# Top-32 attention and an ELU feed-forward block on one core: gates shared between two engines, a written prologue, and weights decoded at another pace

## The chip, the cores and the metric

The kernel runs on one core of a Trainium2 chip. The metric is device time in microseconds (us), from repeated runs of the same program. Five engines work side by side, each through its own queue in order: TensorE (PE, with its weight loads as PEld), VectorE (DVE), ScalarE (ACT), GpSimd (POOL) and SyncE (SP), which issues most DMAs.

## The reference, cut to what matters

There are 8 batches, 8 heads, 576 positions and a head dimension of 64. Each query keeps only its 32 largest scores. The output of attention, 4608 tokens of 512 values, goes through a feed-forward block (FFN) with 2048 hidden values and an ELU between its two products. q, k and v are float32; the weights arrive as float64 words and are turned into float32 on the chip.

```python
scores = scale * np.matmul(q, k.transpose(0, 1, 3, 2))
kth = np.partition(scores, -top_k, axis=-1)[..., -top_k:-top_k + 1]
scores = np.where(scores >= kth, scores, -1000000000.0)
scores = scores - np.max(scores, axis=-1, keepdims=True)
attn = np.exp(scores)
attn = attn / (np.sum(attn, axis=-1, keepdims=True) + 1e-09)
x = np.matmul(attn, v)        # heads side by side: (4608, 512)
...
h = x @ w_in
g = np.where(h > 0.0, h, np.exp(np.minimum(h, 0.0)) - 1.0)
return g @ w_out
```

## The kernel before

**Steps.** The attention is cut into 144 steps, each one tile of 128 query rows for a pair of heads: per batch four full tiles (`qt` 0 to 3) for four head pairs, and a remainder of 64 rows per head (`qt` 4) in two steps. For one step, `scores` (L291) makes the scores on PE and ACT copies them to SBUF; `select_row` (L313) or `select` (L334) finds the 32nd largest value of each row on DVE, for each of two heads with four MAX8 and three MATCH_REPLACE8 over 576 columns; `mask` (L357) turns scores into weights with POOL's `neg` and `gap` and two ACT passes; `normalise` (L374) divides on POOL; `turn` (L391) transposes on PE, with ACT's copies; `attend` (L416) multiplies by v on PE, and `finish` (L453) copies the result into `xT`, the FFN's input. These parts of one step are spread over the loop's steps: scores are made two steps ahead, mask and normalise come one step later, the turn two steps later.

**Order.** The first eight steps (`tight`, L541) are left to the language's own scheduler, which orders each engine's instructions by priority. From step 8 on the loop is under `manual_schedule` (L666): PE, ACT, DVE and POOL execute in the order in which the program is written, and a step is cut into quarters by `next(passes)`.

**FFN.** Tokens are gathered into 19 blocks of one, two or three slots of 128 tokens. When a block's `xT` is complete, its pieces are queued: 16 `hidden` pieces (L478), each four matmuls into a PSUM tile, two ACT Relu's of it (`n` of the negative part, `g` of the positive), an ACT Exp of `n`, and a gate that has to follow; then four `project` pieces per slot (L507), each four of 16 matmuls. `feed` (L601) is called in every quarter step and lets out as many pieces as a plan of costs and due times asks for, so that PE's FFN work is spread evenly. A piece is held back until the number of decoded weights, `decoded`, is high enough: for block 0 in stages, for every later block until all 32 are decoded.

**Gates.** The gate `g = g + n - 1` completes the ELU. It runs on DVE (L471), put off by `close_gates(2)` in `feed` for two quarters; a `hidden` piece closes the oldest if more than three are open, and a `project` piece closes all. `n` has five buffers (four for block 0).

**Decoding.** Each of 32 weight pieces (128 x 512 float64, 512 KB) is loaded by SP (`load_weight`, L150) into a raw tile of four parts: the low and high words interleaved, `e` and `m`. `convert_first` (L159) runs three ACT passes (L169 to L171) and a POOL clamp (L172); `convert_last` (L176) runs two DVE instructions (L179, L182) and a POOL integer add (L186) into the weight tile. `decode_piece` (L204) loads piece i+2, runs the first half of piece i and the last half of piece i−1. `hook` (L193) takes the next of 33 such pieces. It is called twice for each head's row in steps 0 to 7, four times a step, so that the last piece falls in step 8. When all are done the raw tiles are given up and the FFN's late buffers take their place. Three raw tiles exist.

**Prologue.** Before the loop, q and k of two head pairs are loaded (each six DMAs on SP), with the first two weights in between, and the scores of steps 0 and 1 are made, in the scheduler's order.

Of the kernel before, what the change touches and what calls it, by code (L numbers as in the profile page):

```python
# [12 lines left out]
I32 = mybir.dt.int32  # L13
# [67 lines left out]
def kernel(  # L81
# [27 lines left out]
    def pool(name, bufs, **kw):  # L109
        return ctx.enter_context(tc.tile_pool(name=name, bufs=bufs, **kw))  # L110
# [5 lines left out]
    wkpool = pool("wk", 1)  # L116
    etpool = pool("et", 2)
    small = pool("small", 4)
    xtpool = pool("xt", 2)
    opool = pool("o", 1)  # L120
    ps_sc = pool("ps_sc", 1, space=PSUM)
    ps_t = pool("ps_t", 2, space=PSUM)
# [3 lines left out]
    raws = ExitStack()  # L126
    early = raws.enter_context(tc.tile_pool(name="early", bufs=1))
    earlyf = raws.enter_context(tc.tile_pool(name="earlyf", bufs=4))
    rawpool = raws.enter_context(tc.tile_pool(name="raw", bufs=3))

    ident = const.tile([P, P], FP32, tag="ident", name="ident")
    make_identity(nc, ident[:])
# [15 lines left out]
        return moe_w_out[f * P : (f + 1) * P, :], w_out[:, f, :]  # L148

    def load_weight(i):  # L150
        t = rawpool.tile([P, 4 * WN], U32, tag="raw", name="raw")
        nc.sync.dma_start(t[:, 0 : 2 * WN], weight(i)[0])
        raw[i] = t

    def parts(t):
        words = t[:, 0 : 2 * WN].rearrange("p (n w) -> p n w", w=2)
        return words[:, :, 0], words[:, :, 1], t[:, 2 * WN : 3 * WN], t[:, 3 * WN :]

    def convert_first(i):  # L159

        lo, hi, e, m = parts(raw[i])
        ef, mf = e.bitcast(FP32), m.bitcast(FP32)
        nc.scalar.activation(ef, hi.bitcast(FP32), AF.Abs, scale=2.0**-48)  # L169
        nc.scalar.activation(mf, lo, AF.Copy, scale=2.0**-29, bias=2.0**23)  # L170
        nc.scalar.activation(m.bitcast(I32), mf, AF.Copy, bias=-(2.0**23))  # L171
        nc.gpsimd.tensor_scalar(  # L172
            ef, ef, (2.0 - 2.0**-3 - 2.0**-23) * 2.0**-32, 2.0**-63, ALU.min, ALU.max
        )

    def convert_last(i):  # L176
        t, dst = raw.pop(i), weight(i)[1]
        lo, hi, e, m = parts(t)
        nc.vector.tensor_scalar(  # L179
            e, e, 0x0FFFFFFF, 3, ALU.bitwise_and, ALU.logical_shift_left  # L180
        )
        nc.vector.scalar_tensor_tensor(  # L182
            out=e, in0=hi, scalar=0x80000000, in1=e,
            op0=ALU.bitwise_and, op1=ALU.bitwise_or,
        )
        nc.gpsimd.tensor_tensor(  # L186
            dst.bitcast(I32), e.bitcast(I32), m.bitcast(I32), ALU.add
        )

    decode = []  # L190
# [2 lines left out]
    def hook():  # L193

        if not decode:
            return
        decode.pop(0)()
        if not decode:
            raws.close()
            late["f"] = ctx.enter_context(tc.tile_pool(name="f", bufs=5))  # L200
            late["g"] = ctx.enter_context(tc.tile_pool(name="g", bufs=2))
            late["x"] = ctx.enter_context(tc.tile_pool(name="x", bufs=2))

    def decode_piece(i):  # L204
        if i < 2 * NF:
            if i + 2 < 2 * NF:
                load_weight(i + 2)
            convert_first(i)
        if i > 0:
            convert_last(i - 1)  # L210
            decoded[0] = i

    loaded, kqT, vT = {}, {}, {}

    def load_qk(b, hp):

        for name, src in (("k", k), ("q", q)):
            n = J + 1 if name == "k" else J
            t = ldpool.tile([P, n, 2, D], FP32, tag=name + "in", name=name + "in")
            if name == "k":  # L220
                last = t
            for hh in range(2):
                nc.sync.dma_start(
                    t[:, 0:J, hh, :],
                    src[b, 2 * hp + hh, 0:JP, :].rearrange("(p j) d -> p j d", j=J),
                )
            nc.sync.dma_start(
                last[0:R, J, :, :] if name == "k" else last[R:P, J, :, :],
                src[b, 2 * hp : 2 * hp + 2, JP:S, :].rearrange("h p d -> p h d"),
            )  # L230
            loaded[b, hp, name] = t
# [47 lines left out]
    def start_qk(b, hp):  # L279
        turning.append(transpose_qk(b, hp))  # L280
# [32 lines left out]
    def select_row(u, i):  # L313
        if i == 0:
            u.first = small.tile([P, 2, 8], FP32, tag="m1", name="m1")
            u.last = small.tile([P, 2, 8], FP32, tag="m4", name="m4")
        sc = u.sc[:, i, :]
        m = u.first[:, i, :]
        nc.vector.max(m, sc)
        wk = wkpool.tile([P, S], FP32, tag=f"wk{i}", name="wk")  # L320
        cur = sc
        for r in range(TOP_K // 8 - 1):
            nc.vector.match_replace(wk[:], m, cur, TAKEN)  # L323
            cur = wk[:]
            if r < TOP_K // 8 - 2:
                m = small.tile([P, 8], FP32, tag=f"m{i}", name="m")[:]
            else:
                m = u.last[:, i, :]
            nc.vector.max(m, cur)  # L329
            if r != 1:  # L330
                hook()
                yield

    def select(u):  # L334

        u.first = small.tile([P, 2, 8], FP32, tag="m1", name="m1")
        u.last = small.tile([P, 2, 8], FP32, tag="m4", name="m4")
        cur = [u.sc[:, i, :] for i in range(2)]
        found = [u.first[:, i, :] for i in range(2)]
        for i in range(2):  # L340
            nc.vector.max(found[i], cur[i])  # L341
        yield
        wk = [wkpool.tile([P, S], FP32, tag=f"wk{i}", name="wk")[:] for i in range(2)]
        for r in range(TOP_K // 8 - 1):
            for i in range(2):
                nc.vector.match_replace(wk[i], found[i], cur[i], TAKEN)  # L346
            cur = wk
            for i in range(2):
                if r < TOP_K // 8 - 2:
                    found[i] = small.tile([P, 8], FP32, tag=f"m{i}", name="m")[:]  # L350
                else:
                    found[i] = u.last[:, i, :]
                nc.vector.max(found[i], cur[i])  # L353
            hook()
            yield
# [96 lines left out]

    def finish(blk, parts, at, cols, src):  # L453
        if blk.xT is None:
            if blk.slots == 1 and late:
                blk.xT = late["x"].tile([P, NC, P], FP32, tag="xT", name="xT")
            else:
                blk.xT = xtpool.tile([P, NC, T], FP32, tag="xT", name="xT")
        nc.scalar.copy(blk.xT[:, at, cols], src)
        blk.left -= parts  # L460
        if blk.left == 0:
            ffn.extend(ffn_pieces(blk))
# [1 line left out]
    gates = []  # L464
    place = [0]

    def close_gates(keep=0):

        while gates and gates[0][0] <= place[0] - keep:
            _, dst, n = gates.pop(0)  # L470
            nc.vector.scalar_tensor_tensor(  # L471
                out=dst, in0=n, scalar=-1.0, in1=dst, op0=ALU.add, op1=ALU.add
            )

    def ffn_pieces(blk):
        n_tok = blk.slots * P

        def hidden(f):  # L478
# [4 lines left out]
                g = late["g"].tile([P, NG, T], FP32, tag="g", name="gT")  # L483
                blk.gT.append(g[:])
            if len(gates) > 3:
                gates[0] = (-1, *gates[0][1:])
                close_gates(place[0])
            ps = ps_f.tile([P, dm], FP32, tag="f", name="hps")
            for i in range(NC):
                nc.tensor.matmul(  # L490
# [11 lines left out]
            nc.scalar.activation(n, ps[:, 0:n_tok], AF.Relu, scale=-1.0)  # L502
            nc.scalar.activation(g, ps[:, 0:n_tok], AF.Relu)  # L503
            nc.scalar.activation(n, n, AF.Exp, scale=-1.0)  # L504
            gates.append((place[0], g, n))

        def project(s, part):  # L507
            close_gates()
            if part == 0:
                blk.o = ps_f.tile([P, dm], FP32, tag="f", name="ops")  # L510
            step = NF // 4
            for f in range(part * step, (part + 1) * step):
                nc.tensor.matmul(  # L513
                    blk.o[:],
                    blk.gT[f // NG][:, f % NG, s * P : (s + 1) * P],
                    w_out[:, f, :],
                    start=(f == 0),
                    stop=(f == NF - 1),
                )
            if part == 3:  # L520
                o = opool.tile([P, dm], FP32, tag="osb", name="osb")
                nc.scalar.copy(o[:], blk.o[:])
                for t in blk.tiles[s]:
                    p0 = t.cols.start - s * P
                    nc.sync.dma_start(out[t.rows, :], o[p0 : p0 + t.ql, :])
# [87 lines left out]
            fed["sum"] += cost  # L613
            piece()

    load_qk(0, 0)
    for i in range(2):
        load_weight(i)
    load_qk(0, 1)
    load_v(0, 0)  # L620
    start_qk(0, 0)
    turn_qk(True)
    scores(steps[0])
    load_qk(0, 2)
    start_qk(0, 1)
    turn_qk(True)
    scores(steps[1])
    load_qk(0, 3)
    for hp in range(1, NHP):
        load_v(0, hp)  # L630
    decode += [lambda i=i: decode_piece(i) for i in range(2 * NF + 1)]
    at(0, start_qk, 0, 2)
    at(1, start_qk, 0, 3)

# [5 lines left out]
    for n in range(NS + 3):  # L640
# [20 lines left out]
                feed(n, 0.25)  # L661
            continue
        if n == tight:
            E = mybir.EngineType
            ctx.enter_context(
                tc.manual_schedule(engines={E.PE, E.Activation, E.DVE, E.Pool})  # L666
            )
        passes = select(cur) if cur else iter(range(4))
        if ahead:
            scores(ahead)  # L670
# [59 lines left out]
```

## Time and profile before

| what | us |
|---|---|
| median of 3 runs | 1694.59 (1694.2 to 1695.28) |
| the profiled execution's own time | 1695.23 |
| its span, first to last instruction | 1693.4 |
| busy: PE / DVE / ACT / POOL | 1597.5 / 1542.7 / 1179.6 / 627.0 |
| first MAX8 of step 0 on DVE | 15.91 |
| DVE begins step 9, 10, 11 | 164.43, 174.07, 184.23 |
| gates on DVE (L471) | 304, 129.1 busy |
| weight decoding on DVE (L179, L182) | 64, 45.7 busy |

The profile is of one execution. An engine is counted as busy while it executes; DMA issues, branches and semaphores don't count. Rows of instructions give the line, the engine, the operation, output and input with their shapes, the number, and busy time, mean duration and the idle time before them with what ended it. In views of stretches each line has the stretch, its length and each engine's busy time with its number of instructions, then the granted TensorE clock, the DMA share and GB/s.

### The profile page before, as it was taken

The numbers are of one execution on the slowest core, as the hardware profiler recorded it, in microseconds if no ns is written. First come the engines' busy times: TensorE is split into PE (matmuls) and PEld (weight loads), VectorE is DVE, ScalarE is ACT, GpSimd is POOL, SyncE is SP. The second block draws the span as 40 slices with busy tenths as digits, with TensorE's granted clock in tenths as the row PEclk, the third lists the DMA queues.
The fourth block names the chain that finished last, engine by engine and source line by source line (L and its number), as shares of the span: only waits on it lengthen the run. The fifth ranks groups of instructions, "written<-read, shape, count | busy, mean of one in ns | idle before, by whom it ended". The sixth has DMA issues, their size and how long they took to land.

```text
span 1693.4 us, 26805 instructions
## 1 busy us (share of the span) xinstructions
PE 1597.5 (94%) x8560; PEld 1035.0 (61%) x8560; DVE 1542.7 (91%) x3248; ACT 1179.6 (70%) x2813; POOL 627.0 (37%) x1719
## 2 busy tenths in 40 slices
PE   4568899999999999999999999999999999999999
PEld 3355676667575666756557575755557575755565
DVE  6889999999999999999999999999998999998600
ACT  5787776778776776857758585867758686857531
POOL 3675333343333333433333333333333333332200
PEclk8568999999999999999999999999999999999999
DMA  5531021001200111001100111001100000000000
GB/s 156 169 130 63 15 56 36 7 1 42 51 12 7 29 35 42 1 14 42 43 19 1 28 42 35 7 10 46 36 20 8 21 21 28 7 7 7 7 13 13
DMA packets 101131, 56.25 MB, mean 33 GB/s; under 512 B 84096, under 2 KB 92288, under 8 KB 100992
## 3 DMA queue, kind: packets, MB, share of 16 engines
q1 hardware_dynamic: 100992, 54.55, 11.7%
q8 instruction: 68, 1.11, 0.3%
q14 instruction: 71, 0.58, 0.1%
HBM read 45.09 MB, written 9.44 MB: 32 GB/s over the span
## 4 chain that ended last, share of the span: by engine, by line
PE 68%; DVE 21%; ACT 5%; issue 2%; POOL 2%; DMA 1%; SPq 0%; ACTq 0%; POOLq 0%; DVEq 0%
PE ops L513 25%; PE hps L490 21%; PE avps L432 8%; DVE wk L346 7%; PE scps L300 7%; DVE m L353 6%; PE eps L406 5%; DVE m L341 2%; DVE gT L471 1%; DVE wk L323 1%; DVE m L329 1%; PE qkps L270 1%; ACT sc L370 1%; ACT sc L369 1%; ACT et L407 1%
## 5 line engine op out<-in xcount | busy, mean ns | idle before, releaser
L353 DVE MAX8 m<-wk 128x8 f32<-128x576 f32 x816 | 574.9, 745 | 0.0
L490 PE MATMUL hps<-xT,w_in 128*128 128x256 f32 (+2 forms) x2432 | 554.3, 376 | 19.3 <-ACT gT L503 19.3
L513 PE MATMUL ops<-w_out,gT 128*128 128x512 f32 x1152 | 522.6, 598 | 0.0
L490 PEld LDWEIGHTS hps<-xT,w_in 128*128 128x128 f32 x2432 | 409.5, 194 | 119.9 <-ACT gT L503 26.4
L346 DVE MATCH_REPLACE8 wk<-m,wk 128x576 f32<-128x576 f32 x544 | 399.4, 741 | 0.0
L513 PEld LDWEIGHTS ops<-w_out,gT 128*128 128x128 f32 x1152 | 208.4, 190 | 232.8 <-issue 201.0
L380 POOL TENSOR_SCALAR dene<-den 128x2 f32<-128x2 f32 x144 | 34.9, 243 | 819.6 <-ACT sc L370 819.0
L369 ACT ACTIVATE sc<-sc,neg 128x576 f32<-128x576 f32 x288 | 226.5, 787 | 56.6 <-POOL neg L366 56.1
L370 ACT ACTIVATE sc<-sc,gap 128x576 f32<-128x576 f32 x288 | 223.2, 775 | 26.6 <-ACT sc L369 1.9
L308 ACT ACTIVATE sc<-scps 128x576 f32<-128x576 f32 x288 | 173.4, 661 | 82.4 <-PE scps L300 82.4
L387 POOL TENSOR_SCALAR sc<-sc,rec 128x576 f32<-128x576 f32 x288 | 218.7, 769 | 15.2 <-POOL rec L385 0.4
L300 PE MATMUL scps<-kqT 64*128 64x288 f32 (+1 forms) x1280 | 198.1, 438 | 21.5 <-ACT sc L308 14.7
L471 DVE SCALAR_TENSOR_TENSOR gT<-n,gT 128x256 f32<-128x256 f32 (+2 forms) x304 | 129.1, 431 | 95.3 <-ACT n L504 95.3
L407 ACT COPY et<-eps 128x512 f32<-128x512 f32 x288 | 167.4, 581 | 61.8 <-PE eps L406 61.8
L406 PEld LDWEIGHTS eps<-ident,sc 128*128 128x128 f32 x1152 | 144.5, 145 | 93.4 <-issue 48.9
L346 DVE MATCH_REPLACE8 wk<-m,sc 128x576 f32<-128x576 f32 x272 | 199.7, 741 | 0.0
L432 PE MATMUL avps<-et,vT 128*64 128x256 f32 (+2 forms) x2080 | 191.0, 325 | 9.0 <-ACT et L407 8.4
L406 PE MATMUL eps<-ident,sc 128*128 128x128 f32 x1152 | 177.9, 280 | 21.8 <-POOL sc L387 18.6
L341 DVE MAX8 m<-sc 128x8 f32<-128x576 f32 x272 | 191.3, 744 | 0.0
L432 PEld LDWEIGHTS avps<-et,vT 128*64 128x64 f32 x2080 | 122.3, 140 | 80.4 <-issue 24.7
L502 ACT ACTIVATE n<-hps 128x256 f32<-128x256 f32 (+2 forms) x304 | 112.6, 370 | 84.2 <-PE hps L490 79.0
L300 PEld LDWEIGHTS scps<-kqT 64*128 64x128 f32 (+1 forms) x1280 | 106.0, 180 | 90.2 <-issue 45.1
(47 smaller groups left out, 1236.6 us busy)
## 6 DMA issues: line engine op xcount, KB each, us to landing
kin<-in_k_dram SPq DMA_DIRECT2D x64, 128.0 KB, 2.8
qin<-in_q_dram SPq DMA_DIRECT2D x64, 128.0 KB, 2.8
raw<-in_moe_w_in_dram SPq DMA_DIRECT2D x16, 512.0 KB, 3.9
vT<-in_v_dram SPq DMA_DIRECT2D x64, 128.0 KB, 2.3
raw<-in_moe_w_out_dram SPq DMA_DIRECT2D x16, 512.0 KB, 3.3
out_dram<-osb SPq DMA_DIRECT2D x32, 256.0 KB, 2.2
kin<-in_k_dram SPq DMA_DIRECT2D x32, 32.0 KB, 2.5
kin<-in_q_dram SPq DMA_DIRECT2D x32, 32.0 KB, 2.2
```

The source lines that it names most:

```text
L300: nc.tensor.matmul(wide[i][rows, half, 0:HS], kq[part, q0 : q0 + u.t.ql], kq[part, k0 : k0 + HS], start=True, stop=True,)
L341: nc.vector.max(found[i], cur[i])
L346: nc.vector.match_replace(wk[i], found[i], cur[i], TAKEN)
L353: nc.vector.max(found[i], cur[i])
L369: nc.scalar.activation(sc, sc, AF.Prelu, bias=neg[:], alpha=STEEP)
L370: nc.scalar.activation(sc, sc, AF.Exp, bias=gap[:], accum_out=u.den[:, i : i + 1])
L387: nc.gpsimd.tensor_scalar(u.sc[:, i, :], u.sc[:, i, :], rec[:, i : i + 1], 1.0, ALU.mult, ALU.mult)
L406: nc.tensor.transpose(ps[:, c * P : (c + 1) * P], sc[:, c0 : c0 + P], ident[:])
L407: nc.scalar.copy(g.et[:, chunks, u.at, :], ps[:, 0 : n * P].rearrange("p (c q) -> p c q", c=n),)
L432: nc.tensor.matmul(ps[i * D : (i + 1) * D, cols], vt[:, 2 * J + i if c == J else i * J + c, :], w, start=(c == 0), stop=(c == J),)
L490: nc.tensor.matmul(ps[:, 0:n_tok], w_in[:, i, f * P : (f + 1) * P], blk.xT[:, i, 0:n_tok], start=(i == 0), stop=(i == NC - 1),)
L513: nc.tensor.matmul(blk.o[:], blk.gT[f // NG][:, f % NG, s * P : (s + 1) * P], w_out[:, f, :], start=(f == 0), stop=(f == NF - 1),)
```

## The change

- Every second gate, those with an odd number `f`, runs on POOL as two instructions. A `project` piece closes only the gates that it reads, and a full list closes only its oldest. `n` has four late buffers in place of five.
- The prologue's transposes and first scores of steps 0 and 1 are under `manual_schedule`, before the other q and k loads; q of the first head pair is loaded from ACT's queue; the second weight is loaded after the second head pair.
- A raw tile has three parts: the `m` values are written in place of the low words. There are five raw tiles, and the last half of a piece runs two pieces after its first half.
- In the first four steps (`qt` 0) a row has one hook in place of two; `select` has four in place of three. There are 34 pieces.
- `xT` of a one-slot block comes from a pool of three small buffers from the start; the wide ones are made when decoding has ended.

```diff
-    rawpool = raws.enter_context(tc.tile_pool(name="raw", bufs=3))
+    rawpool = raws.enter_context(tc.tile_pool(name="raw", bufs=5))
...
-        t = rawpool.tile([P, 4 * WN], U32, tag="raw", name="raw")
+        t = rawpool.tile([P, 3 * WN], U32, tag="raw", name="raw")
...
-        return words[:, :, 0], words[:, :, 1], t[:, 2 * WN : 3 * WN], t[:, 3 * WN :]
+        return words[:, :, 0], words[:, :, 1], t[:, 2 * WN :]
...
-        lo, hi, e, m = parts(raw[i])
-        ef, mf = e.bitcast(FP32), m.bitcast(FP32)
+        lo, hi, e = parts(raw[i])
+        ef, mf = e.bitcast(FP32), lo.bitcast(FP32)
...
-        nc.scalar.activation(m.bitcast(I32), mf, AF.Copy, bias=-(2.0**23))
+        nc.scalar.activation(lo.bitcast(I32), mf, AF.Copy, bias=-(2.0**23))
...
-            dst.bitcast(I32), e.bitcast(I32), m.bitcast(I32), ALU.add
+            dst.bitcast(I32), e.bitcast(I32), lo.bitcast(I32), ALU.add
...
-            late["f"] = ctx.enter_context(tc.tile_pool(name="f", bufs=5))
+            late["f"] = ctx.enter_context(tc.tile_pool(name="f", bufs=4))
...
-        if i > 0:
-            convert_last(i - 1)
-            decoded[0] = i
+        if i > 1:
+            convert_last(i - 2)
+            decoded[0] = i - 1
...
             if r != 1:
-                hook()
+                if r > 1 or u.t.qt > 0:
+                    hook()
                 yield
...
             nc.vector.max(found[i], cur[i])
+        hook()
         yield
...
-            if blk.slots == 1 and late:
-                blk.xT = late["x"].tile([P, NC, P], FP32, tag="xT", name="xT")
+            if blk.slots == 1:
+                blk.xT = xpool.tile([P, NC, P], FP32, tag="xT", name="xT")
...
-    def close_gates(keep=0):
+    def close_gates(keep=0, upto=None):
-        while gates and gates[0][0] <= place[0] - keep:
-            _, dst, n = gates.pop(0)
-            nc.vector.scalar_tensor_tensor(
-                out=dst, in0=n, scalar=-1.0, in1=dst, op0=ALU.add, op1=ALU.add
-            )
+        while gates:
+            put, group, dst, n = gates[0]
+            if put > place[0] - keep if upto is None else group > upto:
+                return
+            gates.pop(0)
+            if group[1] % 2 == 0:
+                nc.vector.scalar_tensor_tensor(
+                    out=dst, in0=n, scalar=-1.0, in1=dst, op0=ALU.add, op1=ALU.add
+                )
+            else:
+                nc.gpsimd.tensor_scalar_add(n, n, -1.0)
+                nc.gpsimd.tensor_tensor(dst, dst, n, ALU.add)
...
-            close_gates()
+            close_gates(upto=(blk.number, (part + 1) * NF // 4 - 1))
...
-    load_qk(0, 0)
-    for i in range(2):
-        load_weight(i)
+    load_qk(0, 0, nc.scalar)
+    load_weight(0)
     load_qk(0, 1)
+    load_weight(1)
     load_v(0, 0)
-    start_qk(0, 0)
-    turn_qk(True)
-    scores(steps[0])
+    with tc.manual_schedule(engines=engines):
+        for hp in range(2):
+            start_qk(0, hp)
+            turn_qk(True)
+            scores(steps[hp])
     load_qk(0, 2)
-    start_qk(0, 1)
-    turn_qk(True)
-    scores(steps[1])
     load_qk(0, 3)
...
-    decode += [lambda i=i: decode_piece(i) for i in range(2 * NF + 1)]
+    decode += [lambda i=i: decode_piece(i) for i in range(2 * NF + 2)]
```

More of the change, by code (lines that the diff above doesn't have):

```diff
@@ L118 @@
     small = pool("small", 4)
-    xtpool = pool("xt", 2)
+    xpool = pool("x", 3)
     opool = pool("o", 1)
@@ L177, in convert_last @@
         t, dst = raw.pop(i), weight(i)[1]
-        lo, hi, e, m = parts(t)
+        lo, hi, e = parts(t)
         nc.vector.tensor_scalar(
@@ L199, in hook @@
             raws.close()
-            late["f"] = ctx.enter_context(tc.tile_pool(name="f", bufs=5))
+            late["f"] = ctx.enter_context(tc.tile_pool(name="f", bufs=4))
             late["g"] = ctx.enter_context(tc.tile_pool(name="g", bufs=2))
-            late["x"] = ctx.enter_context(tc.tile_pool(name="x", bufs=2))
+            late["x"] = ctx.enter_context(tc.tile_pool(name="xt", bufs=2))
     def decode_piece(i):
@@ L208, in decode_piece, with load_qk @@
             convert_first(i)
-        if i > 0:
-            convert_last(i - 1)
-            decoded[0] = i
+        if i > 1:
+            convert_last(i - 2)
+            decoded[0] = i - 1
     loaded, kqT, vT = {}, {}, {}
-    def load_qk(b, hp):
+    def load_qk(b, hp, other=nc.sync):
         for name, src in (("k", k), ("q", q)):
-            n = J + 1 if name == "k" else J
+            n, queue = (J + 1, nc.sync) if name == "k" else (J, other)
             t = ldpool.tile([P, n, 2, D], FP32, tag=name + "in", name=name + "in")
@@ L222, in load_qk @@
             for hh in range(2):
-                nc.sync.dma_start(
+                queue.dma_start(
                     t[:, 0:J, hh, :],
@@ L226, in load_qk @@
                 )
-            nc.sync.dma_start(
+            queue.dma_start(
                 last[0:R, J, :, :] if name == "k" else last[R:P, J, :, :],
@@ L454, in finish @@
         if blk.xT is None:
-            if blk.slots == 1 and late:
-                blk.xT = late["x"].tile([P, NC, P], FP32, tag="xT", name="xT")
+            if blk.slots == 1:
+                blk.xT = xpool.tile([P, NC, P], FP32, tag="xT", name="xT")
             else:
-                blk.xT = xtpool.tile([P, NC, T], FP32, tag="xT", name="xT")
+                blk.xT = late["x"].tile([P, NC, T], FP32, tag="xT", name="xT")
         nc.scalar.copy(blk.xT[:, at, cols], src)
@@ L485, in hidden @@
             if len(gates) > 3:
-                gates[0] = (-1, *gates[0][1:])
-                close_gates(place[0])
+                close_gates(upto=gates[0][1])
             ps = ps_f.tile([P, dm], FP32, tag="f", name="hps")
@@ L504, in hidden @@
             nc.scalar.activation(n, n, AF.Exp, scale=-1.0)
-            gates.append((place[0], g, n))
+            gates.append((place[0], (blk.number, f), g, n))
         def project(s, part):
-            close_gates()
+            close_gates(upto=(blk.number, (part + 1) * NF // 4 - 1))
             if part == 0:
@@ L614, in feed @@
             piece()
-    load_qk(0, 0)
-    for i in range(2):
-        load_weight(i)
+    E = mybir.EngineType
+    engines = {E.PE, E.Activation, E.DVE, E.Pool}
+    load_qk(0, 0, nc.scalar)
+    load_weight(0)
     load_qk(0, 1)
+    load_weight(1)
     load_v(0, 0)
-    start_qk(0, 0)
-    turn_qk(True)
-    scores(steps[0])
+    with tc.manual_schedule(engines=engines):
[3 more added lines that the diff above has]
+            scores(steps[hp])
     load_qk(0, 2)
-    start_qk(0, 1)
-    turn_qk(True)
-    scores(steps[1])
     load_qk(0, 3)
@@ L663 @@
         if n == tight:
[L664 to L667, printed above, removed]
+            ctx.enter_context(tc.manual_schedule(engines=engines))
         passes = select(cur) if cur else iter(range(4))
```

## The prediction

> **What bounds the kernel now.** I read in this order: the tenths of the page, the busy times in stretches, who waited for whom, then the timeline around the places that this brings up. The tenths say that two engines are full for different parts of the run.
>
> ```profile
> PE   4568899999999999999999999999999999999999
> DVE  6889999999999999999999999999998999998600
> ACT  5787776778776776857758585867758686857531
> POOL 3675333343333333433333333333333333332200
> PEclk8568999999999999999999999999999999999999
> ```
>
> The same in stretches of my choosing (length, then busy time and instructions of PE, weight load, DVE, ACT, POOL). 184.23 is where DVE begins step 11 (its two L341 MAX8), 712.57 a later step's start, 1588 about its end.
>
> ```profile
> 38.00:158.00 120.00, 77.92 (x386) 55.85 (x385) 108.67 (x202) 94.41 (x217) 82.83 (x126) 0.69 0.41 128
> 184.23:712.57 528.34, 506.28 (x3168) 349.66 (x3168) 528.34 (x1146) 395.98 (x1007) 197.50 (x586) 1.00 0.10 26
> 712.57:1588.00 875.43, 869.80 (x4421) 542.00 (x4420) 843.05 (x1774) 623.39 (x1431) 314.94 (x918) 1.00 0.08 22
> ```
>
> So there are three regimes. Up to about 158 us the weights are decoded, no engine is full, and DVE is nearest to it (108.67 of 120). From 184 to 713 DVE has no idle time at all (528.34 of 528.34), while PE lacks 22.1 us. From 713 on PE lacks 5.6 us of 875 and DVE has 32 us to spare. Since PE executes its queue in order and the feeder puts the same work at the same place of it, the end time is PE's work plus PE's idle time: whatever lets PE reach 713's place earlier is kept to the end, and nothing more is to be had after it except stalls. The waits show how the full DVE reaches PE: through the mask, POOL's `neg` and ACT's queue.
>
> ```profile
> POOL neg L366 <- DVE m L353: 31.4, 42, 2.8
> ACT sc L369 <- POOL neg L366: 16.1, 16, 3.0
> PE hps L490 <- ACT gT L503: 13.4, 18, 1.6
> ```
>
> (184 to 712 us: total, times, longest.) The last is a hidden matmul waiting for ACT to free its PSUM buffer, mostly in the one-slot blocks.
>
> **What the Trainium skill says.** "GPSIMD Engine Reference", section 3.1, gives 4497 ns for a two-input fp32 add of 2048 elements, 2.2 ns an element, against half of it on DVE. The trace agrees: L186 took 1270 ns at 512 elements (2.5 ns), L471 on DVE 424 ns at 256 (1.7). "SBUF — State Buffer", section "SBUF: two separate sides", says that a GpSimd instruction and a DVE instruction with two SBUF inputs or in a two-port mode exclude each other for the whole instruction. The trace agrees: L179 needs 400 ns at least but 1.49 us when it meets L186:
>
> ```profile
> 52.45 1.27 POOL L186 TENSOR_TENSOR w_in<-raw 128x512 int32<-128x512 int32 x1
> ```
>
> ```profile
> 52.52 1.49 DVE L179 TENSOR_SCALAR raw<-raw 128x512 uint32<-128x512 uint32 x1 [0.51 <-POOL raw L172]
> ```
>
> MAX8 and MATCH_REPLACE8, DVE's main load, aren't touched: 733 to 760 ns for L353 between 150 and 420 us, beside whatever POOL did. "DMA: Bandwidth & Descriptors", section "Issuing engines are not separate DMA queues", says that a second issuing engine saves only issue time; that is all I credit the move of q to ACT's queue with.
>
> **The change, part by part.**
>
> *Place of the work.* I replayed the feeder's arithmetic for both versions: hidden and project pieces fall into the same quarter steps, except one project part of block 0, one step later. Of 304 gates 289 (285 before) close two quarters after their hidden piece, 11 in the tail because more than three are open, 4 (8 before) at a project. Decoding has 34 pieces: 8 in steps 0 to 3, 16 in steps 4 to 7, then 4, 4 and 2; it ends in step 10, two steps later than now. Every later FFN piece needs all weights, but block 1 is only ready in step 10, so PE loses nothing by that.
>
> *Start.* Now DVE's first MAX8 comes at 15.91. PE could begin only at 6.77, when q's last part, issued at 4.14, had landed; and ACT's first kqT copy stood until 10.41 behind a weight decode that waited for its DMA:
>
> ```profile
> 9.85 0.66 ACT L169 ACTIVATE raw<-raw 128x512 f32<-128x512 f32 x1 [7.85 <-DMA raw<-in_moe_w_in_dram]
> 10.41 0.30 ACT L263 COPY kqT<-scps 128x192 f32<-128x192 f32 x1
> ```
>
> The written prologue puts no decoding there. From PE's 6.77: copies from about 7.5 to 9.2, scores 2.3, sc copy 0.66, so DVE starts near 12. Three DMA issues on ACT (0.63 to 0.7 each) lie before anything it could do.
>
> *Decoding, five buffers, half pace.* I count DVE up to step 11, as it is the tightest. Its busy time up to 184.2, added from 20 us stretches, is 158.2, its idle time 26.0: 12.7 before 15.9, 13.3 after. The waits put 25.2 of the idle on L179 waiting for POOL's L172 (11.2 of it the first one). Two pieces of lag between first and last half give that chain a quarter to half a step more, and a load no longer waits for the last POOL add of the piece just ahead (SP stood 67.4 us for POOL's L186). The DVE, ACT and POOL instructions per piece stay the same in number, so busy stays 158.2, less 8 of block 0's 16 gates, which cost up to 1.23 us there because of the port, some 0.6 on average: 153. With 12 idle at the start and 0 to 13.3 after it, step 11 begins at 165 to 178.5; I take 10, as ACT is busy 131 and POOL 105 of the same 184 us and will be in each other's way: 175. Gain 9 (6 to 19). That covers SP too: the first weights after the prologue are still queued behind the same q, k and v issues (28.5 us now), but steps 0 to 3 ask for half as many.
> The unknown is the strided access: low words are now written and read in place, 8 bytes apart. ACT shows strided 673 and 666 ns against 620 dense, that is 0.05 us; POOL's add with one strided input has no row. Below: nothing, the two-input read is the limit. Above: doubled, 1.27 us × 32 = 41 us of POOL. POOL's load over steps 4 to 10 would be about 4 us a step for normalise and masks and 4 × 1.9 for decoding, 12 with gates of some 16 us a step; the add would have to exceed about 2.2 us before POOL binds. I take nothing.
>
> *Gates.* Half of 304 leave DVE; each becomes an add with a constant and a two-input add on POOL. From L172 (612 ns at 512) and L186: 0.31 + 0.64 to 0.4 + 0.75, so about 1.0 us at 256, 0.6 at 128, 1.5 at 384, together about 88 × 1.0 + 40 × 0.6 + 24 × 1.5 = 148 us. POOL goes from 37% to 46%. What hides it: POOL idles 5 to 7 us a step waiting for ACT's exponentials:
>
> ```profile
> POOL dene L380 <- ACT sc L370: 819.0, 138, 11.5
> ```
>
> Gates that come in that wait are free. One placed after normalise delays `neg` of the next mask by up to 1.5 us; around 1002 us ACT takes `neg` 1.0 us after it is there, and PE turns the tile 1.9 to 3.7 us after normalise ended. The projects need a gate some 10 us after it is issued.
> What it brings: from step 11 to 712.57 are 51 steps; a step without gates takes 9.64 (174.07 less 164.43), 491.6 in all, so gates cost DVE 36.7 there. Half is 18. The stretch is then 510, and PE's own work is 506.3; late now is PE. Both cannot fit perfectly, and the one-slot hidden pieces wait for ACT anyway, so I take 14 (8 to 18). After 713 nothing.
>
> *Buffers.* `n` goes from five to four, so in 10 of the hidden pieces of blocks 1 to 4 ACT's L502 would reuse a buffer whose gate was issued in the same quarter (none now). Four of those gates are on POOL, behind a normalise of 3.4 us at worst: 4 × 3.4 = 14 us of ACT, with 25% of ACT free and DVE two steps ahead; up to 3 us for PE, inside the 14. In the tail 12 reuses wait 1 us for a gate that is done while PE works 1.5 us a piece: nothing. `xT` has three small buffers for one-slot blocks and two late wide ones: no place is later than now.
>
> *Sum.* 1695.23 (the profiled execution: span 1693.4 and 1.8 around it) − 9 − 14 = 1672.2. The median shown is 0.64 lower: 1671.6.
>
> **Rivals.**
> B, the front gives nothing (three engines in each other's way, DVE idle as much as now), and PE stays with half of its stalls: −2 and −7, about 1686. For it: ACT's and POOL's load in that stage. Against: the lag takes away just the wait that the trace names.
> C, no change: the relief of DVE is all returned as PE waits for ACT in the one-slot blocks and front and buffers cancel: 1694. For it: the 13.4 us of hidden matmuls waiting for ACT. Against: DVE at 100% there.
> D, slower: POOL's pairs come into PE's path after 713, where PE is full and gains nothing. About 75 gates there move to POOL at 1.2 us (256 and 384 mixed); if a third of them delay mask or normalise past the slack, PE loses 30 us, and the sum is 1695 − 23 + 30, about 1702. It decides from 23 us on, a quarter of the pairs. For it: slacks of only 1 to 4 us. Against: no wait of PE for POOL in that stage and POOL 36% busy.
>
> **How the numbers follow.** Forecast 0.60 (its own range 1661 to 1681), B 0.16, C 0.08, D 0.16. The forecast's lower edge has both gains near their ends, −19 and −17: 1659. To leave out no more than two in ten the range goes to 1694. 0.2% is 3.4 us, about what a measurement here can tell: faster (below 1691.2) 0.77, same 0.07, slower 0.16.
>
> **What would show it.** Right: first MAX8 near 12 us, step 11 near 175; then steps of about 10.0 us on DVE with gaps in it before 700 us, PE idle of some 8 in place of 22 in that stretch; 304 more POOL instructions at about 0.3 and 0.65 us; DVE's busy time near 1480. Wrong: an L186 above 2 us, PE or ACT waiting for a POOL gate, decoding that ends after 185 us, or PE idle after 713 grown by more than a few us.

## The result, and the profile after

The changed kernel takes 1711.34 us (median of 4 runs, 1709.71 to 1712.86), the kernel before beside it 1694.93. The ratio is 1.0097, 95% interval 1.0079 to 1.0114: slower by 16 us where I had forecast 23 less. The profiled execution took 1710.78, its span is 1709.0.

The tenths of the page after:

```profile
PE   6686899999999999999999999999999999999999
DVE  6989899999999999998999989898997989897600
ACT  6876776778676776867758585867758686767531
POOL 3786544554555454645536354645535445554521
```

DVE is full in far fewer slices, so the relief came; POOL rose from 37% to 50%, more than the 46% that I had reckoned with; and PE's row looks as before although the run is longer. Two readings say where the time went. The first compares the same piece of PE's work in both kernels, from ACT's copy of output slot 10 to that of slot 29 (slots are explained below; stretch, length, busy PE, PEld, DVE, ACT, POOL, then clock, DMA share, GB/s); the kernel before first:

```profile
663.36:1507.05 843.69, 838.22 (x4389) 534.14 (x4388) 817.58 (x1725) 610.30 (x1415) 309.37 (x901) 1.00 0.08 22
```

```profile
670.89:1522.56 851.67, 842.11 (x4389) 532.68 (x4388) 794.26 (x1653) 610.12 (x1415) 430.35 (x1045) 1.00 0.08 22
```

DVE does 23 us less and POOL 121 us more, and the same 4389 matmuls take 8.0 us longer. PE's idle time grew from 5.5 to 9.6 us and its busy time by 3.9. Part of that busy time is waiting too, since the profile counts a short wait inside a row of matmuls as busy. Twenty `avps` matmuls of the kernel before and of the changed one, from PE's timelines (start, duration):

```profile
1009.91 2.38 PE L432 MATMUL avps<-et,vT 128*64 128x256 f32 x20
```

```profile
1020.02 2.92 PE L435 MATMUL avps<-et,vT 128*64 128x256 f32 x20
```

In the changed kernel ACT's copy of the last part of `et`, which these matmuls read, ends only at 1020.50, inside the row. The second reading is who waited for whom, over the whole run (total, times, longest), in the kernel before and in the changed one:

```profile
ACT sc L369 <- POOL neg L366: 56.1, 46, 3.3
```

```profile
ACT sc L372 <- POOL neg L369: 103.7, 57, 5.9
...
PE ops L524 <- POOL w_out L187: 15.1, 6, 5.3
```

ACT's wait for `neg` nearly doubled. In the changed kernel 37 of these 57 waits, 66.9 of the 103.7 us, come when a gate's pair of POOL instructions stands directly ahead of the `neg` in POOL's queue. PE's wait for the weight decoding wasn't there at all before.

DVE's start of a step turned out to be a bad measure of progress, because DVE can run up to two steps ahead of PE. A better one is ACT's copy of a finished output slot (`osb`), of which there are 36, numbered from 0: PE has then done all that is ahead of it. The times before, and how much later (+) each kernel is, from the ACT timelines:

| slot | before, us | changed | gates all on DVE | gates alone on POOL | POOL third quarter | POOL fourth quarter | no gates | neg first |
|---|---|---|---|---|---|---|---|---|
| 0 | 168.59 | +8.44 | +6.16 | +4.70 | +6.29 | +6.46 | +1.32 | +7.03 |
| 1 | 223.62 | +4.04 | +0.53 | +5.09 | +2.82 | +4.13 | −4.31 | +1.21 |
| 4 | 384.07 | +3.87 | −0.63 | +8.87 | +1.66 | +3.24 | −5.46 | +0.46 |
| 10 | 663.36 | +7.53 | +0.37 | +12.35 | −0.40 | +5.59 | −7.52 | −1.21 |
| 18 | 1037.05 | +10.64 | −1.88 | +15.35 | −4.17 | +6.57 | −11.28 | −4.91 |
| 27 | 1423.56 | +14.34 | −2.84 | +20.86 | −5.13 | +11.71 | −12.25 | −5.81 |
| 35 | 1689.60 | +15.51 | −2.85 | +21.99 | −5.14 | +13.22 | −12.26 | −5.82 |

In the changed kernel the first output slot is 8.4 us late, 4 of which stay, and from 384 us on the lag grows by about 1 us in 100 us until the steps end. The other columns are the experiments below.

One place where a pair delays a mask, from the timelines of POOL and ACT (start, duration, engine, line, operation), first in the kernel before and then, at the same place of the work, in the changed one:

```profile
1022.30 1.48 POOL L387 TENSOR_SCALAR sc<-sc,rec 128x576 f32<-128x576 f32 x2
1023.74 0.23 POOL L366 TENSOR_SCALAR neg<-m 128x1 f32<-128x1 f32 x1
...
1024.01 0.78 ACT L369 ACTIVATE sc<-sc,neg 128x576 f32<-128x576 f32 x1 [0.85 <-POOL neg L366]
```

```profile
1032.67 1.48 POOL L390 TENSOR_SCALAR sc<-sc,rec 128x576 f32<-128x576 f32 x2
1034.12 0.87 POOL L484 TENSOR_SCALAR n<-n 128x256 f32<-128x256 f32 x1
1035.07 0.72 POOL L485 TENSOR_TENSOR gT<-gT,n 128x256 f32<-128x256 f32 x1
1035.77 0.23 POOL L369 TENSOR_SCALAR neg<-m 128x1 f32<-128x1 f32 x1
...
1036.03 0.78 ACT L372 ACTIVATE sc<-sc,neg 128x576 f32<-128x576 f32 x1 [2.23 <-POOL neg L369]
```

Before, `neg` follows normalise at once. In the changed kernel normalise ends at 1034.15, the gate's pair comes next, and `neg` starts 1.6 us later. ACT, whose mask needs `neg`, stands idle for 2.23 us in place of 0.85, and the exponentials, the next normalise and PE's turn come after that mask.

### The profile page after: what moved, and what is told of

Same layout as the page of the kernel before. It is cut to its first block, busy times and chain, and to the rows that moved or that the text cites. A ratio compares the mean times of both kernels' runs of the same rounds, so it can differ in the third digit from the quotient of the medians.

```text
span 1709.0 us, 26875 instructions
## 1 busy us (share of the span) xinstructions
PE 1612.8 (94%) x8560; PEld 1038.9 (61%) x8560; DVE 1494.3 (87%) x3096; ACT 1181.2 (69%) x2813; POOL 857.2 (50%) x2023
## 4 chain that ended last, share of the span: by engine, by line
PE 68%; ACT 16%; POOL 9%; issue 3%; DVE 3%; DMA 1%; SPq 0%; ACTq 0%; POOLq 0%
PE ops L524 28%; PE hps L501 17%; PE avps L435 9%; PE scps L301 7%; PE eps L409 5%; ACT sc L372 4%; ACT sc L373 4%; ACT et L410 2%; POOL sc L390 2%; ACT n L513 1%; POOL n L484 1%; ACT n L515 1%; ACT gT L514 1%; POOL rec L385 1%; POOL gT L485 1%
## 5 line engine op out<-in xcount | busy, mean ns | idle before, releaser
L524 PE MATMUL ops<-w_out,gT 128*128 128x512 f32 x1152 | 528.8, 603 | 15.1 <-POOL w_out L187 15.1
L372 ACT ACTIVATE sc<-sc,neg 128x576 f32<-128x576 f32 x288 | 226.4, 787 | 103.9 <-POOL neg L369 103.7
L390 POOL TENSOR_SCALAR sc<-sc,rec 128x576 f32<-128x576 f32 x288 | 215.2, 758 | 14.9
L480 DVE SCALAR_TENSOR_TENSOR gT<-n,gT 128x256 f32<-128x256 f32 (+2 forms) x152 | 68.5, 450 | 160.4 <-ACT n L515 160.1
L301 PE MATMUL scps<-kqT 64*128 64x288 f32 (+1 forms) x1280 | 193.8, 436 | 13.1 <-ACT kqT L277 7.9
L435 PE MATMUL avps<-et,vT 128*64 128x256 f32 (+2 forms) x2080 | 195.3, 325 | 8.5 <-ACT et L410 8.3
L484 POOL TENSOR_SCALAR n<-n 128x256 f32<-128x256 f32 (+2 forms) x152 | 129.3, 850 | 50.0 <-ACT n L515 49.8
```

Of the source, the lines that this page charges most:

```text
L301: nc.tensor.matmul(wide[i][rows, half, 0:HS], kq[part, q0 : q0 + u.t.ql], kq[part, k0 : k0 + HS], start=True, stop=True,)
L372: nc.scalar.activation(sc, sc, AF.Prelu, bias=neg[:], alpha=STEEP)
L390: nc.gpsimd.tensor_scalar(u.sc[:, i, :], u.sc[:, i, :], rec[:, i : i + 1], 1.0, ALU.mult, ALU.mult)
L435: nc.tensor.matmul(ps[i * D : (i + 1) * D, cols], vt[:, 2 * J + i if c == J else i * J + c, :], w, start=(c == 0), stop=(c == J),)
L524: nc.tensor.matmul(blk.o[:], blk.gT[f // NG][:, f % NG, s * P : (s + 1) * P], w_out[:, f, :], start=(f == 0), stop=(f == NF - 1),)
```

## The experiments

All kernels of a group ran beside the kernel before on one chip, whose median was 1694.68, 1694.84, 1694.28 and 1693.61 us in the four groups.

**All gates on DVE again, the front alone.**

```diff
-            if group[1] % 2 == 0:
+            if True:
```

> The changed kernel with every gate on DVE again; the front and the buffers stay as changed. Theory (the POOL pairs in front of neg delay mask and turn and cost the kernel some 14 us between step 40 and the end, and the front's gain of 27 us at step 7 is given back by step 19): about 1697 us, with steps 12 to 19 near where the changed kernel has them and no growing lag after step 40. Rival (the loss comes from four buffers for n in place of five, or from the later end of decoding): 1708 to 1712, as the changed kernel.

1692.97 us, ratio 0.9995 (0.9986 to 1.0003), 4 us less than I expected. The gates' move costs 18 us, and all the rest of the change together moves nothing that can be measured. Four buffers for `n` and the later end of decoding, which stayed, are not the cause.

**The gates' move alone, on the kernel before.**

```diff
-            nc.vector.scalar_tensor_tensor(
-                out=dst, in0=n, scalar=-1.0, in1=dst, op0=ALU.add, op1=ALU.add
-            )
+            if f % 2 == 0:
+                nc.vector.scalar_tensor_tensor(
+                    out=dst, in0=n, scalar=-1.0, in1=dst, op0=ALU.add, op1=ALU.add
+                )
+            else:
+                nc.gpsimd.tensor_scalar_add(n, n, -1.0)
+                nc.gpsimd.tensor_tensor(dst, dst, n, ALU.add)
```

> The kernel before with nothing changed but the engine of the odd gates, which become the two POOL instructions. Theory: the lag grows from step 40 on as in the changed kernel and the time is 1706 to 1711 us. Rival (relief of DVE is worth what I forecast and the loss is all in the front and the buffers): about 1681.

1715.83 us, ratio 1.0129 (1.0114 to 1.0144), somewhat worse than I expected: 21 us for half of the gates moved, with five buffers for `n` as before. The rival, relief worth what I had forecast, is out.

**Where the pair stands in POOL's queue.** From step 8 on the feeder closes 137 odd gates: 48 in the fourth quarter of a step, 21 in the first, 49 in the second and only 19 in the third. In the first three of these places a `neg` comes next in POOL's queue; in the third it is normalise, which waits for ACT anyway. (POOL's queue in the changed kernel's trace has the same: next after the pair comes `neg` for 118 pairs, normalise for 19.) Two versions put all gates of one quarter on POOL, with r = 3 or r = 0, and every other gate on DVE:

```diff
-            if group[1] % 2 == 0:
+            if upto is not None or place[0] % 4 != r or place[0] <= 4 * tight:
```

> The changed kernel, but from step 8 on a gate goes to POOL exactly if it is closed in the third quarter of a step (62 gates by the written order), where it stands behind the second neg and gap and ahead of normalise, which waits for ACT's exponentials anyway; all others run on DVE. Theory (a POOL pair costs what it delays neg and so ACT's mask): these pairs cost nothing, 1690 to 1694 us, at or under the 1693.0 of the version with all gates on DVE. Rival (the pairs cost by their length or number wherever they stand): 62 of 152 pairs times 18 us are 7 us, so about 1700.

> The same with the fourth quarter (68 gates), where a pair stands between normalise and the first neg of the next step. Theory: nearly the full cost per pair of the changed kernel or more, 1699 to 1706 us, and ACT waiting for neg about 80 us or more in place of 61 with all gates on DVE. Rival (place doesn't matter): the same time as the third-quarter version within 1.5 us.

Third quarter, 62 pairs: 1689.8 us, ratio 0.9970 (0.9959 to 0.9981), faster than before. Fourth quarter, 68 pairs of the same three widths: 1707.95, ratio 1.0079 (1.0064 to 1.0094), a little over what I expected. The two versions are 18 us apart, and their pairs differ by only 8 us of POOL's time (99 and 107): the place decides. The wait of ACT for `neg` in the third-quarter version, then in the fourth-quarter version:

```profile
ACT sc L372 <- POOL neg L369: 49.6, 38, 8.5
```

```profile
ACT sc L372 <- POOL neg L369: 96.6, 54, 8.5
```

**The same 152 pairs, but neg and gap first.** The pairs are as many and as long as in the changed kernel; only POOL's order differs.

```diff
         if prev:
             normalise(prev)
+        if cur:
+            for i in range(2):
+                cur.bound[i] = bounds(cur, i)
         feed(n, 0.25)
...
+    def bounds(u, i):
+        low, top = u.last[:, i, 7:8], u.first[:, i, 0:1]
+        neg = small.tile([P, 1], FP32, tag="neg", name="neg")
+        nc.gpsimd.tensor_scalar_mul(neg[:], low, -1.0)
+        gap = small.tile([P, 1], FP32, tag="gap", name="gap")
+        nc.gpsimd.tensor_tensor(gap[:], low, top, ALU.subtract)
+        return neg, gap
...
+        neg, gap = u.bound.pop(i) if i in u.bound else bounds(u, i)
```

> The changed kernel with all its 152 POOL pairs, but neg and gap of a step are issued on POOL right behind the normalise before them, ahead of the pairs of the fourth, first and second quarter, so that no pair stands between a step's last MAX8 and its neg. Theory (the delay of neg is the cost): 1688 to 1695 us, ACT's wait for neg back to 60 us or less in place of 104. Rival (the pairs cost through normalise or through late gates): 1704 to 1711.

And the same order with all gates on DVE, to see what the order is worth without them:

> The same order of neg and gap with all gates on DVE, as the measure for it. Theory: nothing stands in front of neg there, so 1692 to 1695 us, the 1693.0 of that version within 2 us. Rival (the early neg is worth something by itself): under 1691.

1689.18 us, ratio 0.9972 (0.9962 to 0.9982), and 1691.64, ratio 0.9985 (0.9978 to 0.9991). So 22 us of the changed kernel come back by order alone. In this kernel one wait for `neg`, of 1.6 us, is left that directly follows a pair, and the total is the least but for the version without gates:

```profile
ACT sc L378 <- POOL neg L364: 45.4, 31, 4.4
```

With neg first, half of the gates on POOL bring 2.5 us over all of them on DVE; the early neg by itself brings about 1 us over the 1692.97 of the first experiment, which is too little to be told from nothing.

**The length of the pair.** Two versions change the first of the two POOL instructions: in one it adds minus one and then zero, in the other it multiplies by one twice, so that the minus one is not computed.

```diff
-                nc.gpsimd.tensor_scalar_add(n, n, -1.0)
+                nc.gpsimd.tensor_scalar(n, n, -1.0, 0.0, ALU.add, ALU.add)
...
-                nc.gpsimd.tensor_scalar_add(n, n, -1.0)
+                nc.gpsimd.tensor_scalar(n, n, 1.0, 1.0, ALU.mult, ALU.mult)
```

> The changed kernel with the first POOL instruction of a gate written with two operations (add -1, add 0) in place of one. In the changed kernel the one-operation form took 876 ns at 256 columns, while two-operation forms of POOL took 612 ns at 512. Theory (length of the pair is what delays neg): the instruction falls to about 0.35 us, a third of the pair, and 5 to 8 us come back: 1703 to 1706. Rival (any POOL work there costs a fixed hand-over, not its length; or the form isn't what makes it slow): 1709 to 1712.

> The changed kernel with the first POOL instruction of a gate as a multiplication by one, twice, in the form that normalise and nothing else here uses; the ELU's minus one isn't computed. Its two additions took 1093 ns at 256 columns and its one addition 876, while normalise's two multiplications take 758 at 576. Theory (POOL's addition with a constant is the slow operation, and the length of the pair counts): about 0.35 us at 256 columns, the pairs shorter by 80 us in all, and the time 4 to 9 us under the changed kernel's 1711.3. Rival (the tile or the place makes it slow, or only the number of pairs counts): 0.85 us or more, 1709 to 1713.

The two additions gave 1715.07 us (ratio 1.0123, 1.0108 to 1.0138), slower and not faster: neither alternative of that expectation. The multiplications gave 1699.1 (ratio 1.0032, 1.0020 to 1.0045), 12 us less than the changed kernel, more than I expected. The groups at 256 columns (busy, mean ns of one), in the changed kernel, with two additions, and with two multiplications:

```profile
L484 POOL TENSOR_SCALAR n<-n 128x256 f32<-128x256 f32 x88 | 77.1, 876 | 39.3 <-ACT n L515 39.3
```

```profile
L484 POOL TENSOR_SCALAR n<-n 128x256 f32<-128x256 f32 x88 | 96.2, 1093 | 37.6 <-ACT n L515 37.6
```

```profile
L484 POOL TENSOR_SCALAR n<-n 128x256 f32<-128x256 f32 x88 | 36.0, 409 | 43.6 <-ACT n L515 43.6
```

Not the one-operation form is slow but the addition. Summed over all shapes, both instructions of the pairs, POOL spent 168 us on gates with multiplications, 238 in the changed kernel and 268 with two additions, and the times stand 6, 18 and 22 us above the version with all gates on DVE. In this place the length of the pair is paid for, about 0.12 to 0.17 us for each added microsecond.

**What DVE's relief can be worth.** The version with all gates on DVE, without the gate instructions:

```diff
-                nc.vector.scalar_tensor_tensor(
-                    out=dst, in0=n, scalar=-1.0, in1=dst, op0=ALU.add, op1=ALU.add
-                )
```

> The version with all gates on DVE, with the gate instructions left out: the ELU's last addition isn't computed, everything else is. Theory (from step 11 to 60 PE's work and its hand-overs with ACT set the pace, and DVE's full time there isn't what holds the kernel): step 60 begins less than 6 us before the 690.6 of the version with gates, and the time is 1685 to 1692 us. Rival (DVE sets the pace there, as I forecast): the 36 us of gates come out of the stretch up to PE's own idle time, step 60 near 672 to 678 and the time 1670 to 1680.

1684.29 us, ratio 0.9946 (0.9931 to 0.9961): 8.7 us under the version with the gates, and just under the range that I expected. My expectation failed in its marker: step 60 began 27 us earlier on DVE (663.1), as the rival had it. But slot 10, output at about that time, came only 7.9 us earlier than with gates on DVE, and 4.8 of these are there at slot 0 already. Between slots 1 and 10 the same 2620 matmuls took 3.0 us less (views of stretches, gates on DVE first, then no gates):

```profile
224.15:663.72 439.57, 421.13 (x2620) 287.10 (x2619) 435.47 (x941) 324.55 (x819) 165.84 (x495) 1.00 0.11 29
```

```profile
219.31:655.84 436.53, 419.18 (x2620) 285.89 (x2619) 420.56 (x870) 324.31 (x819) 160.26 (x494) 1.00 0.11 29
```

DVE's idle time there rose from 4 to 16 us, and PE's stayed near 18. DVE, freed of its gates, ran ahead within the two steps of slack, and PE kept most of its pace. With no gate at all the relief is worth at most 9 us: the granted clock was 0.977 to 0.981 in these runs and 0.973 to 0.978 in those with the gates, and what part of the 9 us is due to that was not separated. Half of the gates can hardly bring more, and brought 2.5.

**The front.** Full pace in steps 0 to 3, with the gates as changed and with all on DVE:

```diff
-                if r > 1 or u.t.qt > 0:
-                    hook()
+                hook()
```

> The changed kernel with two hooks for each row in steps 0 to 3 too, so that decoding has ended in step 8, nearly all of it in the part that the scheduler orders. Theory (the front's gain is lost because decoding and block 0's projects meet in the written order of steps 8 to 11, where PE stood 15.1 us for POOL's weight add): no PE wait for the weight add, step 12 begins 5 to 10 us earlier than the changed kernel's 192.6, and the time is 1702 to 1706. Rival (half pace is what gives the front its gain): steps 4 to 8 as late as before, step 12 at 195 or later, 1710 to 1714.

> Full decoding pace in steps 0 to 3 and all gates on DVE: the rest of the front alone. Theory (with gates on DVE that engine bounds steps 11 to 60 and only the loss in steps 8 to 11 differs): step 12 near 191, no PE wait for the weight add, and 1689 to 1693 us. Rival (half pace is worth something by itself): 1694 to 1697.

1708.53 us (ratio 1.0087, 1.0070 to 1.0104) and 1694.03 (ratio 0.9999, 0.9990 to 1.0007). Full pace takes 2.8 us off the changed kernel, less than I expected and with overlapping intervals, and with gates on DVE adds about 1: no gain or loss by half pace itself is shown. PE doesn't wait for the weight add at full pace, as expected, but step 12 begins at 191.1 and 194.1 us, later than I expected in both.

Block 0's project pieces held back for four quarters after their weights, with half pace and all gates on DVE:

```diff
+            stamp[i - 1] = place[0]
...
-            (PROJECT, max(behind, NF + (part + 1) * NF // 4),
+            (PROJECT, behind or NF + (part + 1) * NF // 4 - 0.5,
...
-        while ffn and decoded[0] >= ffn[0][1] and 0.5 * ffn[0][0] <= fed["over"]:
+        while (
+            ffn
+            and decoded[0] >= ffn[0][1]
+            and 0.5 * ffn[0][0] <= fed["over"]
+            and place[0] - stamp.get(ffn[0][1] + 0.5, -9) >= 4
+        ):
```

> The version with all gates on DVE, half pace kept, with block 0's project pieces let out four quarters after their weights' last half was issued. Theory (PE's stand of 18.4 us for the weight add in the written order is what gives back the front's gain of 24 us at step 8): that wait goes under 4 us, step 12 begins at 180 to 186 in place of 189.9, and the end comes 1 to 5 us earlier than 1693.0. Rival (decoding itself fills POOL, ACT and DVE in steps 8 to 11 and PE's wait only shows it): step 12 within 2 us of 189.9, the end within 2 us of 1693.0.

1691.66 us, ratio 0.9983 (0.9975 to 0.9990), 1.3 under the version without the hold, with overlapping intervals. PE's 18.4 us of waiting for the weight add are down to 0.9, but step 12 begins at 192.1, later than its 189.9, and in place of the old wait there is this one (PE, 108 to 200 us):

```profile
PE eps L411 <- POOL sc L392: 12.5, 2, 9.8
```

PE's stand moved from the weight to the next thing that POOL owes it, normalise. So the wait for the weight is not what gives the front's gain back. That decoding as such fills these steps, as the rival had it, fits this but is not shown.

## Why the prediction was wrong, by its steps

*What bounds the kernel.* That PE's queue order carries every delay to the end held only late in the run: the changed kernel's lag stays at 15.5 us from slot 29 on, but of its 8.4 us at slot 0 only 4.0 are left at slot 1. That DVE's full time between 184 and 713 us was what held the kernel there did not hold. In the kernel without gates DVE has 33 us less to do from step 11 to step 60 (474.9 us busy in place of 507.6), and PE's work between slots 1 and 10 takes 3.0 us less. A full engine that feeds a buffer can be full because it is just about as fast as the rest.

*Gates, the step that failed.* The text said that POOL's wait for the exponentials hides the pairs, that "gates that come in that wait are free", and put the exception, a pair between normalise and `neg`, down to slack. The runs show the exception to be the rule: 118 of 137 pairs close ahead of a `neg`. I had replayed the feeder for the number of gates and the quarter of each hidden piece, but not for the quarter in which they close, which was the number that decides. Neg's slack of 1.0 us, read at one place, is less than a pair. With `neg` ahead of the pairs, all 152 of them cost nothing.

*The size of the pair.* I took 1.0 us at 256 columns from L172 and L186; it is 0.88 + 0.74, and 238 us in all in place of 148. The error is in the first instruction: L172's minimum and maximum were taken as the price of an addition. The second instruction is as I took it from L186 (0.64 to 0.75). With the multiplications the pair is 1.14 us, near my price, and the loss falls from 18 to 6 us. So the mis-sized term is worth some 12 us, but only in this place: with `neg` first the pairs of full length lose nothing. (My text also let DVE's 1.7 ns an element agree with half of POOL's 2.5; it is two thirds. No number rests on it.)

*What the relief brings, the second step that failed.* Forecast 14, at most 9 with no gate anywhere, and 2.5 measured where the pairs do no harm. Result and forecast are 39 us apart: 32 are the gates (14 forecast as gain, 18 lost), and some 7 the front (9 forecast, 2 or nothing measured).

*Start.* Forecast: DVE starts near 12. It started at 15.72 (15.91 before). The prologue was written in order, but the first weights' decoding, written later, still went ahead of it in ACT's queue; the written order doesn't hold for what stands outside of it. In the changed kernel's timeline, ACT:

```profile
8.61 0.66 ACT L170 ACTIVATE raw<-raw 128x512 f32<-128x512 f32 x1 [4.55 <-DMA raw<-in_moe_w_in_dram]
...
10.42 0.31 ACT L264 COPY kqT<-scps 128x192 f32<-128x192 f32 x1
```

q landed earlier, and PE began at 5.99 in place of 6.77, yet ACT's copy came at 10.42 as before.

*Decoding.* Forecast: step 11 at 175, gain 9. It was 179.6, and step 12 at 192.6 against 195.1. Step 7 began 27 us earlier, with DVE idle for 1.5 us from its start on. Most of this was work put off and not saved: at full pace, with gates on DVE, that step begins at 131.8, 3 us earlier than before. Steps 7 to 11, with the rest of the decoding, gave it back (from the start of step 7 to that of step 12, in the changed kernel):

```profile
108.00:192.64 84.64, 61.56 (x315) 41.72 (x314) 70.44 (x136) 57.03 (x139) 55.78 (x93) 0.78 0.24 78
```

DVE was idle for 14.2 us here with no engine full. I had costed the later end of decoding at nothing because block 1 is only ready in step 10. That holds for block 1; block 0's project pieces, though, are let out as soon as the last half of their weights is issued, not done, and PE stood 15.1 us for it. Holding them back took this wait away and brought step 12 no earlier, so what sets the pace of these steps stays open. The strided add cost nothing, as taken: L187 1.29 us at the median, 1.27 before.

*Buffers.* Right: ACT waited 0.8 us in one case for a POOL gate's buffer.

*Rivals.* D was the one that came, in its mechanism. Its place and cost came in part: against the version with gates on DVE the changed kernel loses 7.2 us up to slot 10 (663 us) and 11.2 after it, where D had 30 after 713. Its sum of 1702 lies near the result by luck: it kept my gains of 23, and with the 2 that the runs leave at most it would have been 1723. The argument against it, that PE had no wait for POOL in that stage and POOL was 36% busy, was no evidence: a queue in order is late by what stands in front, however idle it is on average.

The best versions here are the changed kernel with neg and gap first (1689.18) and the one with POOL gates in the third quarter only (1689.8), 0.3% under the kernel before; the two can't be told apart. The kernel with neg first and block 0's projects held as well was not tried.

## What to carry to other kernels

Work moved to an idle engine can cost by what stands behind it in that engine's queue, whatever the engine's share: list for every moved instruction which instruction comes next there, and who waits for that. An engine at 100% is the bound only if removing work from it moves the end; measure progress at the output, since an engine that may run ahead through buffers shows gains that aren't there. Put the short instruction that others wait for ahead of the long one that nobody waits for yet.

## What I had not expected of the hardware

On POOL the time of a one-input instruction with constants depends on the operation. At 128, 256 and 384 columns of fp32 one addition took 562, 876 and 1236 ns, two additions 664, 1093 and 1558, two multiplications 304, 409 and 552: 2.6, 3.5 and 1.0 ns for each further column. The addition of two tensors (470, 740, 1034) is cheaper than the addition of a constant. Why was not looked into.
